# Value products of an attention stage in two column tiles, both halves of the heads together

## The chip, the cores and the metric

One core of one Trainium2 chip runs the whole program. The metric is device time in microseconds (us) of one execution. Engines that matter here: TensorE (PE for its matmuls, PEld for its weight loads), VectorE (DVE), ScalarE (ACT), GpSimd (POOL) and SyncE (SP), which starts the DMA transfers.

## The reference

Three blocks follow each other. The first is a gated linear attention over 2 batches, 8 heads, 768 steps and a head size of 40, given as a recurrence:

```python
C = f_stab * C + i_stab * outer(vt, kt)      # per batch and head, 40x40
n = f_stab * n + i_stab * kt
h_tilde = C @ qt
denom = maximum(abs(n . qt), 1.0)
y[t] = sigmoid(o_gate[t]) * h_tilde / denom
```

The second multiplies each token (320 values) by `w_in` (320x1024) with a ReLU, splits the result into u and v, normalises v over its 512 channels, mixes it over the 768 tokens with `w_spatial`, multiplies by u and then by `w_out`. The third mixes each token with the one before it and applies `w_k`, a squared ReLU, `w_v`, and a sigmoid gate from `w_r`. The two large stages behind the attention don't change here.

## The kernel before, in words

**Attention by chunks.** The 768 steps of each batch are cut into 6 chunks of 128. The 12 chunks are worked one after the other, alternating between the batches (`SEQ`); p, from 0 to 11, is the position in that list. A chunk needs, on TensorE: scores of keys against queries (`sc`, L463), two decay matrices (`ld`, L495 or L471 to L475), the product of the queries with the state carried in (`ip`, L570), the update of that state (`sp`, L533), the value products (`av`, L590), and the transpose of the finished result into the layout of the next block (`tp`, L637). The decay matrix goes through an exponential on ACT and is multiplied by the scores on DVE; that gives `dt`, in halves of 4 heads, 128x512 each.

**Value products.** `intra(i, hh)` does one half. For each of 4 heads a matmul has the head's 128x128 block of `dt` as its weights and streams the value columns of that head. Each head has 41 columns (40 values and a one, for the denominator); the slice taken is three heads wide where there are three, 123 columns, and the columns of the two further heads are overwritten by the matmuls that follow. All eight heads of a chunk write one PSUM bank, `av`, and `normalise` reads it. The operands are f32, and each such matmul stands as two passes in the trace.

**Tiles of the array.** The scores have only 40 rows of contraction. The kernel puts heads 0 to 3 on rows 0 to 39 and heads 4 to 7 on rows 64 to 103, and issues their matmuls alternately (L461 to L464), so that they use two row tiles of the array. All other matmuls of this stage but four very small ones use the array whole.

**Fillers.** The first products of the second block are cut into single matmuls and kept in a list, `fillers`: `vp` (8 matmuls of 512 columns for a chunk, L743) and `up` (32 of 256 columns for two chunks, L748). `pull` puts a chunk's `vp` matmuls at the front of that list once its estimate says that their first weights will be there. `w_v` comes in three pieces, `w_v0` to `w_v2`, each split into a high and a low part by DVE, ACT and POOL.

**The order.** The order of the instructions on TensorE, ACT, DVE and POOL is fixed when the program is built. A planner with a clock of its own walks through the tasks of each position (slots 0 to 6: S0 scores and first half's decays, I, T, N0 first half of the value products, X transpose, S1 second half's decays, N1 second half of the value products and `normalise`). `beat(x)` advances that clock by x. After each task it takes a number of fillers (`FILL`). Where it expects a wait and finds no filler it places `heat`, a matmul on junk (`wp`, L363); `HOT` gives a number of junk matmuls to place at a position without waiting, less the fillers at hand.

The functions that the change touches:

Of the kernel before, what the change touches and what calls it, by code (L numbers as in the profile page):

```python
# [18 lines left out]
def tile_mlstm_gmlp_channelmix(  # L19
# [25 lines left out]
    SEQ = [6 * b + c for c in range(6) for b in range(2)]  # L45
    P = 128
    H, D = 8, 40
    DA = D + 1
# [10 lines left out]
    vec, act, pool, pe = nc.vector, nc.scalar, nc.gpsimd, nc.tensor  # L59
# [11 lines left out]
    clock = [0.0]  # L71
# [12 lines left out]
    class Chain:  # L84
# [14 lines left out]
        def eta(self, k):  # L99
            t = self.ready  # L100
            for s in self.steps:
                t = max(t, free.get(s[0], 0.0)) + s[1] + HOP
                if len(s) > 3 and s[3] == k:
                    break
            return t
# [19 lines left out]
    def use(e, cost, t=None):  # L125
        free[e] = max(free[e], clock[0] if t is None else t) + cost
        return free[e]
# [27 lines left out]
    def beat(cost):  # L155
        clock[0] += cost
        advance(clock[0])
# [170 lines left out]
    st = {}  # L328
# [41 lines left out]
    for a in 'f i d o0 o1 q'.split():  # L370
        dict(f=lambda: sync.dma_start(out=fg, in_=f_gate), i=lambda: sync.dma_start(out=ig, in_=i_gate),
             d=lambda: sync.dma_start(out=id_sb, in_=ident), o=lambda: load_o(int(a[1])), q=lambda: load_qk(SEQ[0]))[a[0]]()
# [207 lines left out]
    def intra(i, hh):  # L580
        if hh == 0:
            both = bank(psa, "at", f"av{i}", ("av", i))
            st["av", i] = both[:, :H * DA].rearrange("p (h d) -> p h d", h=H)
            st["spare", i] = both[:, 384:384 + H]
        wait(("A", i, hh))
        av, vt, A = st["av", i], st["vt", i], st.pop(("A", i, hh))
        for h in range(4):

            own_ = slice(4 * hh + h, min(4 * hh + h + 3, H))
            pe.matmul(av[:, own_, :], A[:, h, :], vt[:, own_, :], start=True, stop=True)  # L590
        beat(0.87)

    def normalise(i):
        b, c = divmod(i, NCH)
# [106 lines left out]
    W = {}  # L701
# [94 lines left out]
    fillers = []  # L796

    vq = []

    def pull():  # L800
        if vq and "v" in W and not (fillers and fillers[0][4]) and eta(["w_v0", ("xt", vq[0])]) <= clock[0] + 1.0:
            fillers[:0] = vpart(vq.pop(0))

    def fill(n, lag=1e9):
# [7 lines left out]
    def wait(*keys):  # L812
        while True:
            gap = eta(keys) - clock[0]
            if gap <= 0.02:
                break
            pull()
            if fillers and eta(fillers[0][2]) <= clock[0] + 0.1:
                fill(1)
            elif warm[0] and gap > 0.2:  # L820
                heat(1)
                clock[0] += 0.08
                advance(clock[0])
            else:
                break
        finish(*keys)
# [38 lines left out]
    for a in 'k0 v0 q6 k6 v1 b v2 n'.split():  # L865
        dict(k=lambda: load_kv(SEQ[a != "k0"]), q=lambda: load_qk(SEQ[1]), n=lambda: load_qk(SEQ[2]),
             v=lambda: w_in_load("u", 0, int(a[1])), b=lambda: load(bm_raw, blockmask[:, 0:3 * DA:DA], 2))[a[0]]()
# [34 lines left out]
                                                            in_=dps[:120, :6 * NCH], func=AF.Exp)))  # L902

    FILL = (6, 4, 1, 3, 1, 1, 1, 4)
    HOT = (0, 1, 0, 0, 3, 2, 0)
    todo = []

    def task(name, fn, keys=(), after=(), slot=0, arrive=None, p=0):
        todo.append(dict(name=name, fn=fn, keys=keys, after=set(after), slot=slot, arrive=arrive, p=p))

    def position(p):
        i = SEQ[p] if p < NT else None
        n = SEQ[p + 1] if p + 1 < NT else None
        nn = SEQ[p + 2] if p + 2 < NT else None
        prev = SEQ[p - 1] if p else None

        def s0():
            if p == 3:
                w_in_split("v")
            if p == 7:  # L920
                wsp_half(0, lsp_[0])
            scores(n, 0)
            logd(n, 0)
            if p % 2 == 0 and 2 <= p < NT - 2:
                gate_rows(p // 2 + 1)

        def gates():
            wait(("G1", 0))
            gate_exp("c", 96, G1)
            decays()  # L930

        def st_():
            if p == 2:
                finish(("eg", "c"), ("dec", 0), stall=False)
                gp.release()
                lsp_.append(tc.alloc_tile_pool(name="lsp", bufs=1, side="left", reuse_waits="tile"))
                vec.tensor_scalar(out=omu_sb, in0=mu_sb, scalar1=-1.0, scalar2=1.0, op0=ALU.mult, op1=ALU.add)
            state(i)

        def tr():  # L940
            turn(prev)
            vq.append(prev)
            if p % 2 == 0:
                fillers.extend(upart(p // 2 - 1))

        def s1():
            scores(n, 1)
            logd(n, 1)
            if p + 3 < NT:
                load_qk(SEQ[p + 3])  # L950
            if p in (3, 5):
                finish(("e", n, 0), ("e", n, 1), stall=False)
                open_gate(2 if p == 3 else 4)
                open_gate(3 if p == 3 else 5)
                use("A", 2.6)

        def n1():
            intra(i, 1)
            normalise(i)
            if nn is not None:  # L960
                load_kv(nn)
            if p == 0:
                w_in_load("v", 1, 0)
                sync.dma_start(out=mu_sb, in_=mu)
            if p == 1:
                w_in_load("v", 1, 1)
                load_o(2)
                load_o(3)
            if p == 2:
                w_in_load("v", 1, 2)  # L970
                load_o(4)
            if p == 3:
                load_o(5)
            if n is not None:
                key_weights(n)

        if n is not None:
            task(("S0", n), s0, after=[("N1", prev), ("S1", i)], arrive=n, slot=0, p=p)
        if p == 0:
            task("B", lambda: (wait(("G0", 1)), gate_exp("b", 16, GC[1])), [("G0", 1)], slot=7, p=p)  # L980
        if p == 2:
            task("G", gates, [("G1", 0)], p=p, slot=7)
        if i is not None:
            c = i % NCH
            if c > 0:
                task(("I", i), lambda: inter(i), [("C", i - 1)], [("N1", prev)], slot=1, p=p)
            if c < NCH - 1:
                task(("T", i), st_, [("kw", i)], [("I", i), ("N1", prev)] + ["G"] * (p >= 2), slot=2, p=p)
            task(("N0", i), lambda: intra(i, 0), [("A", i, 0)], [("S0", i), ("N1", prev)], slot=3, p=p)
        if prev is not None:  # L990
            task(("X", prev), tr, [("x", prev)], [("N1", prev), ("X", SEQ[p - 2] if p > 1 else None)], slot=4, p=p)
        if n is not None:
            task(("S1", n), s1, after=[("S0", n)], slot=5, p=p)
        if i is not None:
            task(("N1", i), n1, [("A", i, 1)], [("N0", i), ("I", i), ("T", i), ("S1", n), ("X", SEQ[p - 2] if p > 1 else None)], slot=6, p=p)

    lsp_ = []
    for p in range(NT + 1):
# [5 lines left out]
    while todo:  # L1004
        p = todo[0]["p"]
# [26 lines left out]
        passed.add(best["name"])  # L1032
        hot = HOT[p] if p < len(HOT) else 0
        if best["slot"] < 7:
# [315 lines left out]
```

## Time and profile before

| what | value |
|---|---|
| median of 3 runs | 307.42 us (305.56 to 309.02) |
| profiled execution | 305.26 us |
| its span, first to last instruction | 303.5 us |
| PE busy | 295.1 us, 2020 matmul passes |
| ACT, DVE, POOL busy | 172.5, 217.4, 139.4 us |
| attention stage with fillers | up to about 112 us of the span |
| value products | 192 passes, 12.6 to 108.4 us |

A matmul's recorded time is its latency; matmuls overlap, so what a pass costs is read from the distance between starts. The chain of waits is followed back from the last instruction: where a row of it names PE, nothing but PE's own queue set the time there. "Granted clock" is the share of TensorE's full clock.

### The profile page before, as it was taken

The page shows a single profiled execution, that of the slowest core. Times are in us where ns is not written, and L with a number is a line of the kernel's source. Part 1 is how long each engine was busy: PE and PEld are TensorE (multiplying, and loading weights), DVE is VectorE, ACT ScalarE, POOL GpSimd, SP SyncE. Part 2 cuts the span into 40 slices and gives each one's busy share as a digit, 9 for nine tenths or more (in the row PEclk, how much of TensorE's full clock was granted, in tenths as well). Part 3 has the DMA queues.
Part 4 walks back from the last instruction along what each step waited for, and adds up shares of the span by engine and source line. Part 5 has one row for each costly group of instructions (what it writes and reads, how often), then busy time and mean ns, then how long its engine had stood idle before and what let it go on. Part 6 is the DMA issues. An engine that isn't in the chain of part 4 may idle for free.

```text
span 303.5 us, 5569 instructions
## 1 busy us (share of the span) xinstructions
PE 295.1 (97%) x2020; PEld 280.5 (92%) x2020; DVE 217.4 (72%) x440; ACT 172.5 (57%) x383; POOL 139.4 (46%) x167
## 2 busy tenths in 40 slices
PE   8998998998999999999999999999999999999994
PEld 6887986887889989999999999999999999999994
DVE  7869997656787768566789989898766665654601
ACT  4675596787655446633354644686926835825600
POOL 5234445447777655615647527485415305303500
PEclk9999999999999999999999999999999999999998
DMA  5979754333343301463124303321010010010001
GB/s 162 305 216 314 245 179 144 82 107 115 94 141 107 107 2 44 128 213 123 43 71 154 114 1 89 92 81 46 1 65 2 0 45 22 0 45 22 1 24 44
DMA packets 13939, 28.76 MB, mean 95 GB/s; under 512 B 2407, under 2 KB 7783, under 8 KB 13911
## 3 DMA queue, kind: packets, MB, share of 16 engines
q1 hardware_dynamic: 13879, 28.33, 29.9%
q8 instruction: 16, 0.26, 0.3%
q0 software_dynamic: 32, 0.07, 0.2%
q14 instruction: 12, 0.10, 0.1%
HBM read 26.20 MB, written 1.97 MB: 93 GB/s over the span
## 4 chain that ended last, share of the span: by engine, by line
PE 87%; ACT 4%; DVE 4%; issue 2%; POOL 1%; DVEq 0%; POOLq 0%; ACTq 0%
PE spp L662 16%; PE kp L662 15%; PE vv L662 14%; PE wop L662 7%; PE up L662 7%; PE vp L662 6%; PE rp L662 5%; PE av L590 5%; PE sc L463 3%; PE wp L363 3%; PE ip L570 2%; PE sp L533 1%; PE ld L495 1%; PE tp L637 1%; ACT vr L731 1%
## 5 line engine op out<-in xcount | busy, mean ns | idle before, releaser
L1193 POOL TENSOR_TENSOR sq<-sq 128x384 f32<-128x384 f32 x32 | 29.9, 941 | 47.9 <-ACT sq L1192 47.9
L662 PE MATMUL spp<-wsp,vn 128*128 128x384 f32 x288 | 50.4, 334 | 0.0
L662 PEld LDWEIGHTS spp<-wsp,vn 128*128 128x128 f32 x288 | 49.9, 188 | 0.0
L662 PE MATMUL kp<-xk,wk 128*128 128x384 f32 x256 | 45.3, 334 | 0.0
L662 PEld LDWEIGHTS kp<-xk,wk 128*128 128x128 f32 x256 | 44.5, 188 | 0.0
L662 PE MATMUL vv<-wv,k 128*128 128x320 f32 x288 | 42.9, 309 | 0.0
L662 PEld LDWEIGHTS vv<-wv,k 128*128 128x128 f32 x288 | 42.4, 188 | 0.0
L235 DVE TENSOR_TENSOR k<-sq,k 128x384 fp32r<-128x384 f32 x32 | 26.2, 820 | 13.6 <-ACT k L1194 13.6
L662 PE MATMUL up<-xg,w_u 128*128 128x256 f32 x192 | 32.4, 297 | 0.0
L1090 POOL TENSOR_TENSOR vs<-vs,u 128x384 f32<-128x384 f32 x16 | 19.5, 1221 | 23.4 <-DVE vs L1089 22.0
L662 PE MATMUL vp<-w_v,xg 128*128 128x512 f32 x96 | 28.5, 415 | 0.5 <-POOL w_v L235 0.5
L662 PEld LDWEIGHTS up<-xg,w_u 128*128 128x128 f32 x192 | 26.1, 191 | 0.4
L1192 ACT ACTIVATE sq<-kp 128x384 f32<-128x384 f32 x32 | 15.5, 488 | 16.8 <-PE kp L662 14.8
L590 PE MATMUL av<-kvq,dt 128*128 128x123 f32 (+1 forms) x192 | 24.6, 272 | 0.0
L590 PEld LDWEIGHTS av<-kvq,dt 128*128 128x128 f32 x192 | 23.8, 191 | 0.7
L284 DVE SCALAR_TENSOR_TENSOR wbits<-wsq,wbits 128x320 int32<-128x320 int32 (+1 forms) x27 | 20.0, 741 | 4.5 <-ACT wsq L274 3.4
L662 PE MATMUL wop<-gt,wo 128*128 128x384 f32 x128 | 22.8, 334 | 0.0
L662 PEld LDWEIGHTS wop<-gt,wo 128*128 128x128 f32 x128 | 22.2, 188 | 0.0
L1233 DVE TENSOR_TENSOR ob<-rs,vv 128x320 f32<-128x320 f32 x12 | 5.8, 487 | 20.4 <-PE vv L662 19.4
L662 PEld LDWEIGHTS vp<-w_v,xg 128*128 128x128 f32 x96 | 17.1, 190 | 3.4 <-POOL w_v L235 0.8
L288 DVE SCALAR_TENSOR_TENSOR wsq<-wraw,wbits 128x320 int32<-128x320 int32 (+1 forms) x21 | 19.7, 944 | 0.4
L1091 ACT CAST gt<-vs 128x384 fp32r<-128x384 f32 x16 | 8.2, 513 | 17.7 <-POOL vs L1090 17.6
(184 smaller groups left out, 567.2 us busy)
## 6 DMA issues: line engine op xcount, KB each, us to landing
kvq<-in_kvq_dram SPq DMA_DIRECT2D x10, 516.0 KB
qk<-in_qk_dram SPq DMA_DIRECT2D x24, 160.0 KB
wraw<-in_w_k_dram SPq DMA_DIRECT2D x6, 512.0 KB
wraw<-in_w_v_dram SPq DMA_DIRECT2D x8, 320.0 KB
wraw<-in_w_sp_dram SPq DMA_DIRECT2D x12, 192.0 KB
og<-in_o_tok_dram SPq DMA_DIRECT2D x12, 160.0 KB
out_dram<-ob SPq DMA_DIRECT2D x12, 160.0 KB
w_inu<-in_w_in_dram SPq DMA_DIRECT2D x3, 512.0 KB
```

Source lines behind the costliest of these rows:

```text
L235: eng.tensor_tensor(out=out, in0=a, in1=b.bitcast(F32), op=ALU.subtract)
L284: vec.scalar_tensor_tensor(out=t["bits"], in0=t["sq"].bitcast(I32), scalar=3, in1=t["bits"], op0=ALU.logical_shift_left, op1=ALU.bitwise_or)
L288: vec.scalar_tensor_tensor(out=t["sq"].bitcast(I32), in0=t["high"], scalar=SIGN, in1=t["bits"], op0=ALU.bitwise_and, op1=ALU.bitwise_or)
L363: pe.matmul(wp[:, :256], junk[:, :P], junk, start=True, stop=True)
L463: pe.matmul(st["sc", i, x][:, h * P:(h + 1) * P], k_[64 * x:64 * x + D, h, :], q_[64 * x:64 * x + D, h, :], start=True, stop=True)
L570: pe.matmul(ip[:, h0 * DA:(h0 + n) * DA], qt[:n * D, g, :], cs[:n * D, h0 * DA:(h0 + n) * DA], start=True, stop=True)
L590: pe.matmul(av[:, own_, :], A[:, h, :], vt[:, own_, :], start=True, stop=True)
L662: pe.matmul(out[0], l, x, start=j == 0, stop=j == len(prs) - 1)
L1090: ("P", 1.29, lambda: pool.tensor_tensor(out=vs, in0=vs, in1=ut[b][:, d, sl], op=ALU.mult)),
L1091: ("A", 0.51, lambda: act.copy(gt[:, 0], vs)), ("V", 0.7, lambda: sub(vec, gt[:, 1], vs, gt[:, 0])))
L1192: chain(("k2", g, f), ("A", 0.49, lambda: act.activation(out=sq, in_=ps, func=AF.Relu), ("kp", g, f)), ("P", 0.96, lambda: pool.tensor_ten ...
L1193: ("P", 0.96, lambda: pool.tensor_tensor(out=sq, in0=sq, in1=sq, op=ALU.mult)),
```

## The change

From position 3 on, N0 only takes the PSUM bank; the products of both halves are issued in N1, 4 heads and then 4 heads. At every position a head's block of weights is cut into two halves of 64 columns, which go to two column tiles of the array (the outputs at partitions 0 and 64), and the slice that is streamed is 60 columns wide instead of 123 (41 for the last head). `pull` waits for all three pieces of `w_v`, with a margin of 0.2 instead of 1.0. `HOT` asks for two junk matmuls at position 2.

```diff
@@ intra
             st["spare", i] = both[:, 384:384 + H]
+            if SEQ.index(i) >= 3:
+                return
+        elif SEQ.index(i) >= 3:
+            wait(("A", i, 0), ("A", i, 1))
+            products(i, 0)
         wait(("A", i, hh))
-        av, vt, A = st["av", i], st["vt", i], st.pop(("A", i, hh))
-        for h in range(4):
-
-            own_ = slice(4 * hh + h, min(4 * hh + h + 3, H))
-            pe.matmul(av[:, own_, :], A[:, h, :], vt[:, own_, :], start=True, stop=True)
-        beat(0.87)
+        products(i, hh)
+
+    def products(i, hh):
+        av, vt, A = st["av", i].rearrange("p h d -> p (h d)"), st["vt", i].rearrange("p h d -> p (h d)"), st.pop(("A", i, hh))
+        for h in range(4 * hh, 4 * hh + 4):
+
+            own_ = slice(h * DA, min(h * DA + 60, H * DA))
+            for r in (0, 64):
+                pe.matmul(av[r:r + 64, own_], A[:, h % 4, r:r + 64], vt[:, own_], start=True, stop=True)
+        beat(0.6)
@@ pull
-        if vq and "v" in W and not (fillers and fillers[0][4]) and eta(["w_v0", ("xt", vq[0])]) <= clock[0] + 1.0:
+        if vq and "v" in W and not (fillers and fillers[0][4]) and eta(["w_v0", "w_v1", "w_v2", ("xt", vq[0])]) <= clock[0] + 0.2:
@@
-    HOT = (0, 1, 0, 0, 3, 2, 0)
+    HOT = (0, 1, 2, 0, 3, 2, 0)
@@ position
-            task(("N1", i), n1, [("A", i, 1)], [("N0", i), ("I", i), ("T", i), ("S1", n), ("X", SEQ[p - 2] if p > 1 else None)], slot=6, p=p)
+            task(("N1", i), n1, [("A", i, 0), ("A", i, 1)], [("N0", i), ("I", i), ("T", i), ("S1", n), ("X", SEQ[p - 2] if p > 1 else None)], slot=6, p=p)
```

The order on TensorE changes with it. First place: a late position, the fillers being `up`. Before, from the last filler ahead of the first half of the value products to the end of the second:

```order
L662 MATMUL up_1_1220<-xg_681,w_u_149 128x256
L590 MATMUL av_1247<-kvq_1047,dt_0_1087 128x123 x4
L662 MATMUL up_2_1258<-xg_681,w_u_148 128x256
L662 MATMUL up_2_1258<-xg_681,w_u_149 128x256
L662 MATMUL up_2_1258<-xg_681,w_u_148 128x256
L637 MATMUL tp_1263<-id_sb,x_1170 128x128 x3
L662 MATMUL up_2_1258<-xg_681,w_u_148 128x256
L495 MATMUL ld_1_1275<-rl,lt_91 128x512
L662 MATMUL up_2_1258<-xg_681,w_u_149 128x256
L590 MATMUL av_1247<-kvq_1047,dt_1_1153 128x123 x2
L590 MATMUL av_1247<-kvq_1047,dt_1_1153 128x82
L590 MATMUL av_1247<-kvq_1047,dt_1_1153 128x41
```

Now, the same stretch of such a position:

```order
L671 MATMUL up_2_1322<-xg_715,w_u_148 128x256
L671 MATMUL up_2_1322<-xg_715,w_u_149 128x256
L671 MATMUL up_3_1351<-xg_715,w_u_148 128x256
L671 MATMUL up_3_1351<-xg_715,w_u_149 128x256
L646 MATMUL tp_1359<-id_sb,x_1265 128x128 x3
L671 MATMUL up_3_1351<-xg_715,w_u_148 128x256
L495 MATMUL ld_1_1365<-rl,lt_91 128x512
L671 MATMUL up_3_1351<-xg_715,w_u_148 128x256
L599 MATMUL av_1348<-kvq_1129,dt_0_1169 64x60 x8
L599 MATMUL av_1348<-kvq_1129,dt_1_1236 64x60 x6
L599 MATMUL av_1348<-kvq_1129,dt_1_1236 64x41 x2
```

The first half has moved behind the transpose and the second decay matrix, and eight whole-array matmuls have become sixteen of 64 output rows, in one run.

Second place: position 4. Before, from the state update `sp` to the fillers at its end:

```order
L533 MATMUL sp_760<-kvq_586,kw_717 120x123 x2
L533 MATMUL sp_760<-kvq_586,kw_717 80x82
L590 MATMUL av_765<-kvq_586,dt_0_626 128x123 x4
L637 MATMUL tp_778<-id_sb,x_710 128x128 x3
L495 MATMUL ld_1_783<-rl,lt_91 128x512
L497 LDWEIGHTS mask
L497 MATMUL ld_1_783<-mask 128x512
L590 MATMUL av_765<-kvq_586,dt_1_690 128x123 x2
L590 MATMUL av_765<-kvq_586,dt_1_690 128x82
L590 MATMUL av_765<-kvq_586,dt_1_690 128x41
L662 MATMUL vp_721<-w_v_602,xg_388 128x512
L662 MATMUL vp_721<-w_v_603,xg_388 128x512
```

Now, from the last of the junk behind `sp` to the first fillers:

```order
L363 LDWEIGHTS id_sb
L363 MATMUL wp<-id_sb 128x256
L646 MATMUL tp_836<-id_sb,x_759 128x128 x3
L495 MATMUL ld_1_848<-rl,lt_91 128x512
L497 LDWEIGHTS mask
L497 MATMUL ld_1_848<-mask 128x512
L599 MATMUL av_831<-kvq_630,dt_0_686 64x60 x8
L599 MATMUL av_831<-kvq_630,dt_1_725 64x60 x6
L599 MATMUL av_831<-kvq_630,dt_1_725 64x41 x2
L671 MATMUL up_0_886<-xg_715,w_u_148 128x256
L671 MATMUL up_0_886<-xg_715,w_u_149 128x256
```

Three junk matmuls stand before `sp` and six between `sp` and `tp`, where none stood; the six `vp` matmuls that stood at the ends of positions 3 and 4 have moved to position 5 and later, and `up` of the next two chunks takes their place.

In the whole program the junk matmuls go from 56 to 77: five more ahead of the first `tp` and one fewer behind it, eight more at position 2 (four of them ahead of `sp`), nine at position 4.

## Rows read from the trace of the kernel before

**Rows 1.** The page, busy time, share of the span and instructions of each engine.

```profile
PE 295.1 (97%) x2020; PEld 280.5 (92%) x2020; DVE 217.4 (72%) x440; ACT 172.5 (57%) x383; POOL 139.4 (46%) x167
```

**Rows 2.** The page, the chain that ended last, by engine.

```profile
PE 87%; ACT 4%; DVE 4%; issue 2%; POOL 1%; DVEq 0%; POOLq 0%; ACTq 0%
```

**Rows 3.** Stages: start:end, length, busy us (instructions) by engine, granted clock, DMA, GB/s.

```profile
60.40:70.10 9.70, 9.70 (x73) 8.30 (x72) 4.95 (x18) 8.23 (x16) 4.69 (x7) 1.00 0.31 88
88.40:96.70 8.30, 8.30 (x71) 7.71 (x70) 6.85 (x20) 5.24 (x15) 6.38 (x11) 1.00 0.40 125
```

**Rows 4.** The chain, one late position: start us, length us, what.

```profile
88.51 1.09 PE sc L463 x16
89.60 0.43 PE ld L495
...
94.97 0.23 PE ld L495
```

**Rows 5.** PEld's timeline, same position: start, length, line, operands, count.

```profile
88.44 0.97 PEld L463 LDWEIGHTS sc<-qk 40*128 40x128 f32 x16 [0.35 <-issue]
...
92.99 0.98 PEld L590 LDWEIGHTS av<-kvq,dt 128*128 128x128 f32 x8
93.89 0.42 PEld L662 LDWEIGHTS up<-xg,w_u 128*128 128x128 f32 x3
...
95.05 0.97 PEld L590 LDWEIGHTS av<-kvq,dt 128*128 128x128 f32 x8
95.94 0.66 PEld L662 LDWEIGHTS up<-xg,w_u 128*128 128x128 f32 x5
```

**Rows 6.** PEld's timeline, the last load of 80 columns and the next.

```profile
92.81 0.15 PEld L533 LDWEIGHTS sp<-kvq,kw 128*80 128x80 f32 x1
92.88 0.19 PEld L662 LDWEIGHTS up<-xg,w_u 128*128 128x128 f32 x1
```

**Rows 7.** Groups by shape: count, busy us, mean ns of one, idle before.

```profile
L590 PE MATMUL av<-kvq,dt 128*128 128x123 f32 x144 | 20.1, 275 | 0.0
L590 PE MATMUL av<-kvq,dt 128*128 128x41 f32 x24 | 4.2, 262 | 0.0
```

**Rows 8.** Loads by shape, same columns.

```profile
L590 PEld LDWEIGHTS av<-kvq,dt 128*128 128x128 f32 x192 | 23.8, 191 | 0.7
L533 PEld LDWEIGHTS sp<-kvq,kw 128*80 128x80 f32 x20 | 2.5, 149 | 0.0
```

**Rows 9.** The chain, positions 1 and 2, and its return to PE.

```profile
18.36 1.09 PE wp L363 x7
...
20.24 0.48 ACT xg L651
...
29.32 0.80 PE sp L533 x6
```

**Rows 10.** ACT's timeline, the copy that the first `tp` waits for.

```profile
18.96 0.24 ACT L619 COPY x<-x 128x64 f32<-128x64 f32 x1 [0.17 <-DVE x L615]
```

**Rows 11.** PE's timeline: matmuls that waited, with idle time and releaser.

```profile
29.32 0.80 PE L533 MATMUL sp<-kvq,kw 128*120 128x123 f32 x6 [1.44 <-ACT dt L479]
...
47.02 0.47 PE L495 MATMUL ld<-rl,lt 128*128 128x512 f32 x1 [0.56 <-DMA rl<-Lxc]
...
49.33 0.73 PE L662 MATMUL vp<-w_v,xg 128*128 128x512 f32 x2 [0.48 <-POOL w_v L235]
...
72.17 0.49 PE L495 MATMUL ld<-rl,lt 128*128 128x512 f32 x1 [0.88 <-ACT dt L505]
```

**Rows 12.** The chain where it leaves PE between 54 and 72 us.

```profile
54.83 0.60 ACT vr L731
...
71.62 0.51 ACT dt L505
```

**Rows 13.** PE's timeline, the matmuls beside the loads of Rows 5.

```profile
93.11 1.05 PE L590 MATMUL av<-kvq,dt 128*128 128x123 f32 x8
```

**Rows 14.** The chain behind the attention stage.

```profile
126.86 24.96 PE spp L662 x144
```

## The prediction

> **What bounds the kernel now.** I read the engine totals first: PE is busy for 295.1 of 303.5 us, and no other engine is near it [rows 1]. The chain of waits says the same from the other side: 87% of it is PE [rows 2]. So what PE no longer has to do is gained, unless another engine takes over. The stage view shows where that could be: between 88.4 and 96.7 us PE is busy for the whole stage and ACT for 5.24 of 8.30 us, but between 60.4 and 70.1 us ACT has 8.23 of 9.70 [rows 3], and there the chain does leave PE and runs through ACT, from 54.83 to the end of an exponential at 72.13 [rows 12]. It is also off PE, on ACT and DVE, from 20.24 to 29.32 [rows 9]. From 72.17 us to the end no wait on PE of more than 0.2 us stands in its timeline. What follows is unchanged from the spatial product on, which starts at 126.86 [rows 14], when the attention stage and its fillers are through. The granted clock is 1.00 in the stages shown [rows 3].
>
> **What a value product costs now.** The loads of eight passes start at 92.99 and the next matmul's load at 93.89: 0.90 us, 0.112 for a pass. The second half, which ends with slices of 82 and 41 columns, takes 95.94 - 95.05 = 0.89 [rows 5]. A pass with 41 columns is no nearer to the next than one with 123, so it is the load of 128 weight columns that sets the pace; the recorded length of the matmul hardly moves either, 262 against 275 ns [rows 7]. Narrower streams alone would give nothing. A position costs 0.90 + 0.89 = 1.79 us.
>
> **What two tiles can do.** Column tiles occur nowhere in this trace; the nearest rows are the scores, in two row tiles. Their 16 loads take 0.97 us, as long as 8 loads of the whole array, 0.98 [rows 5]: two tiles work side by side, a pair every 0.111 us. They also show what a change of tiling costs: on the chain the scores hold 1.09 us [rows 4], 0.20 more than 8 x 0.111, and the decay matmul behind them holds 0.43 where the one without a change before it holds 0.23 [rows 4]. In and out together cost 0.40 us.
>
> A half block has 64 weight columns. A load of 80 columns is followed by the next after 0.07 us [rows 6], and lasts 149 ns against 191 for 128 [rows 8]; by the first, 64 columns take 0.056 us; by the second, 0.112 - 64 x 42/48 ns = 0.056. The 0.07 is rounded and stands for 0.065 to 0.075, so for 0.052 to 0.060; I take 0.058 us for a pair of passes, if the two column tiles work side by side as the row tiles do. Lower end: 0.052. Upper end: 0.111, the pair of the scores.
>
> - From position 3 on: 16 pairs x 0.058 + 0.40 = 1.33 us for 1.79, a gain of 0.46, nine times: **-4.1 us**.
> - Positions 0 to 2 keep their halves apart and pay the change of tiling twice: 8 x 0.058 + 0.40 = 0.86 for 0.89 or 0.90. Six times: **-0.2 us**. Without the merging of the halves, in other words, the tiles would bring nothing.
>
> **What is given back.** A junk matmul costs 1.09 / 7 = 0.16 us [rows 9], and there are 21 more of them.
> - Five more ahead of the first `tp` and one fewer behind it, 0.6 us. The chain passes this junk and goes on through ACT [rows 9]; the `tp` stands behind the junk and waits for a copy on ACT that ended at 18.96 + 0.24 = 19.20 [rows 10], just before the seventh junk matmul was through, so the added ones can be on the path. I take half: **+0.3**.
> - Four at position 2 ahead of `sp` lie in its wait of 1.44 us [rows 11], which ACT and DVE set: 0. Four behind it, where the chain is back on PE: **+0.6**.
> - Nine at position 4: 1.4 us. They stand where PE waited 0.56 us for a DMA of decay rows, and the six `vp` matmuls that waited 0.48 us for `w_v` have left [rows 11]. These are done later and cost the same there. 1.4 - 0.56 - 0.48: **+0.4**.
> - Positions 5 and 6 give 2 x 0.46 us to a PE that arrives earlier at the wait of 72.17 us, which ACT ends after 0.88 us [rows 11]. ACT's chain [rows 12] stays, and `vp`, with its work on ACT, comes a position later, into the same stretch. I let half be lost: **+0.45**.
>
> The products of the first half now come later, and `normalise` with them only after both; it began behind the second half before too, so nothing on DVE, POOL or in the loads of the next chunk is queued behind a later start. The bank `av` is taken at the same place and freed by the same instruction. The transfers keep their order.
>
> Sum: -4.1 - 0.2 + 0.3 + 0.6 + 0.4 + 0.45 = -2.5 us. The profiled execution took 305.26 us, 303.5 of it span, and lies 2.2 us below the median of 307.42; it would come to 302.8, and against the median I forecast **304.9 us**, -0.8%.
>
> **A rule against it.** The loads of the value products run inside the matmuls before them, on the same 128 rows: loads from 92.99 for 0.98 us [rows 5], matmuls from 93.11 for 1.05 [rows 13]. The Trainium skill, page "TensorE: Matmul & The Clock Gate", section "Part 3: Packing small matmuls — row/col tiling", says that a load overlaps matmuls in flight only where its row group differs from theirs. The two column tiles share all their rows, so that by it a load would stand between the streams. The row just named does not bear the rule out for the whole array; no run here shows it for column tiles. It is the third rival.
>
> **The rivals.**
> 1. Nothing is lost to ACT or to the junk at position 1, and the pairs go at 0.054. For it: PE's timeline has long stretches without a wait, and the order is new around 72 us. Then 0.75 us less is given back and 192 pairs save 0.004 each, 0.8 us: -4.0, **303.4 us**. Chance 0.23.
> 2. The other engines absorb it. For it: ACT at 8.23 of 9.70 us [rows 3], and three `vp` sums pushed into positions 6 and 7. Against: from 80 us on PE alone is on the chain. If positions 3 to 7 give nothing, 5 x 0.46 less the 0.45 already counted, 1.85 us, are lost: -0.7, **306.7 us**. Chance 0.18.
> 3. The tiles don't load side by side. Then 32 passes at 0.058 follow each other: 1.86 + 0.40 = 2.26 for 1.79, +0.47 nine times, and 1.33 for 0.90 in six halves, +0.43 each, together +6.8; with the junk and less of the ACT loss, +8. With pairs at the scores' 0.111 it is 16 x 0.111 + 0.40 = 2.18, +0.39 nine times and +0.39 six times: +5.9, with the junk +7. **About 314 us.** It decides from a pair of 0.072 us on: 192 pairs x 0.0135 use up the 2.5 us. For it: no column tile in the trace. Against: the row tiles, and loads that run under matmuls today. Chance 0.20.
>
> **How the numbers follow.** The forecast has 0.39. A measurement of this kernel can tell about 1%, 3.1 us, from no change. Of the forecast's cases three in ten lie beyond -3.1 us (a pair of 0.055, or half of the give-backs absent), and all of rival 1: faster 0.35. The rest of the forecast and rival 2: same 0.44. Rival 3 and a small part of rival 2: slower 0.21. The range leaves out rival 3. Its low end is rival 1 at 303.4 less the 1.9 us by which the fastest of the three runs lay below the median: 301.5. Its high end is rival 2 with the 1.6 us by which the slowest lay above, and half a us more of junk on the path: 309.
>
> **What would show it.** In the changed profile, loads of the value products should come in pairs a few ns apart, the pairs 0.055 to 0.06 us apart, and the 32 passes of a position should hold 1.1 to 1.2 us on the chain with about 0.2 more on the matmul behind them. A distance of 0.11 us between pairs, or single loads at 0.06, is rival 3. `vp` should no longer wait for `w_v`; a wait on ACT between 65 and 90 us that is longer than 0.88 us is rival 2. The start of the spatial product, 126.86 us now, should come at about 124.4. A granted clock below 1.00 anywhere behind the first few us would make all of this wrong.

## The result and the profile after

The changed kernel takes **308.82 us** (median of 20 runs, 306.29 to 311.15), the kernel before 306.43 (20 runs, 305.56 to 309.02). The ratio is 1.0053, 95% interval 1.0031 to 1.0075: about 1.6 us slower, where 0.8% faster was forecast. The ratio leaves out the two slowest of the 20 runs, 310.99 and 311.15 us, and lies near the quotient of the means of the rest (308.4 and 306.8 us), below that of the two medians. The profiled execution took 308.54 us, with a span of 305.5.

The page, engine totals and the chain by engine:

```profile
PE 294.4 (96%) x2233; PEld 273.3 (89%) x2233; DVE 218.5 (72%) x440; ACT 172.4 (56%) x383; POOL 140.3 (46%) x167
...
PE 71%; DVE 9%; ACT 6%; POOL 5%; DMA 4%; issue 2%; SPq 1%; POOLq 0%; DVEq 0%; ACTq 0%
```

PE has hardly less to do than before and 16 points less of the chain [rows 1, 2]; DVE, ACT, POOL and DMA have taken them. The value products themselves did what was predicted. The chain at a late position (start, length, what):

```profile
97.83 0.23 PE ld L495
98.07 0.12 PE up L671
98.19 1.06 PE av L599 x32
99.25 0.78 PE up L671 x5
100.03 1.09 PE sc L463 x16
```

And the weight loads there, with the loads of both tiles in one row of 32:

```profile
98.11 1.01 PEld L599 LDWEIGHTS av<-kvq,dt 128*64 128x64 f32 x32 [0.25 <-DVE sb L732]
```

Within that row the two loads of a pair start 7 to 8 ns apart and the pairs 0.058 us apart. The 32 passes hold the chain for 1.06 us; the same products held PE for 0.90 + 0.89 us before. So the two column tiles load and stream side by side, and rival 3 is out: its rule, quoted in the prediction from the Trainium skill (page "TensorE: Matmul & The Clock Gate", section "Part 3: Packing small matmuls — row/col tiling"), doesn't hold for column tiles in this trace.

What has changed are the waits. PE's timeline (idle time and releaser in brackets), to be held against [rows 11]:

```profile
27.38 0.48 PE L471 MATMUL ld<-unit,Axb 128*128 128x512 f32 x1 [0.59 <-DVE dt L489]
29.50 0.30 PE L423 MATMUL gpsc<-id_sb,i 96*128 96x96 f32 x1 [0.71 <-DVE i L416]
32.27 0.80 PE L533 MATMUL sp<-kvq,kw 128*120 128x123 f32 x6 [1.22 <-ACT dt L479]
48.29 0.49 PE L363 MATMUL wp<-id_sb 128*128 128x256 bf16 x3 [0.85 <-ACT u L764]
...
77.24 0.50 PE L671 MATMUL vp<-w_v,xg 128*128 128x512 f32 x1 [0.95 <-ACT vr L740]
...
91.64 0.50 PE L671 MATMUL vp<-w_v,xg 128*128 128x512 f32 x1 [0.65 <-ACT u L764]
```

The waits on `w_v` and on the decay rows are gone, and so is the one at 72.17. In their place stand two new ones between 27 and 30 us, and three on ACT's work for the second block (`u`, and `vr` for the normalised half v). The state update of position 2, the first `sp` above, starts at 32.27 instead of 29.32. Part of that is the start of this execution: the first scores stand at 10.12, before at 9.16. Counted from the first scores the update comes 22.2 us later, before 20.2.

That distance, and the one from this update to the first matmul of the spatial product, are what the experiments are read by ("head" and "tail", us, both read from PE's timeline). The clock is the mean granted clock of the profiled execution. Where it is below 0.995 that trace holds a stretch of 3 to 7 us at TensorE's lower level, 1.2 GHz, between 29 and 38 us (e4 a second one from 119 us on); in the others the clock stands at 2.4 GHz from 7 us on until the last few us. "Clock up" counts the runs with a mean granted clock of 0.995 or more, and gives their median less the median of such runs of the kernel before on the same chip (41 of its 75 runs on four chips); for the changed kernel those of its chip are not known.

| kernel | median us | ratio to before, interval | head | tail | clock | clock up: runs, us |
|---|---|---|---|---|---|---|
| before | 306.43 | 1 | 20.2 | 97.4 | 0.997 | 41 of 75 |
| changed | 308.82 | 1.0053 (1.0031 to 1.0075) | 22.2 | 96.7 | 1.000 | 8 of 20 |
| e1 tiles only | 306.58 | 0.9999 (0.9967 to 1.0031) | 20.2 | 96.5 | 0.997 | 2 of 12, -1.0 |
| e3 changed, 0.87 | 303.29 | 0.9905 (0.9869 to 0.9940) | 19.6 | 95.6 | 0.998 | 6 of 6, -2.7 |
| e4 changed, old `pull` | 311.80 | 1.0159 (1.0110 to 1.0208) | 21.2 | 103.8 | 0.981 | 2 of 6, +3.2 |
| e5 changed, no junk at 2 | 308.69 | 1.0067 (1.0039 to 1.0096) | 21.6 | 99.0 | 0.989 | 0 of 7 |
| e10 0.6 early only | 307.56 | 1.0023 (0.9994 to 1.0052) | 21.9 | 95.6 | 0.999 | 4 of 12, 0.0 |
| e11 0.6 late only | 304.23 | 0.9905 (0.9876 to 0.9935) | 19.6 | 96.6 | 0.998 | 6 of 6, -1.9 |
| e12 e3 on the whole array | 306.41 | 0.9982 (0.9962 to 1.0001) | 20.0 | 97.6 | 1.000 | 12 of 12, +0.3 |
| e13 e3, no junk at 2 | 303.19 | 0.9884 (0.9854 to 0.9914) | 19.7 | 95.6 | 0.999 | 5 of 6, -3.0 |
| e14 before with 0.6 | 313.84 | 1.0240 (1.0218 to 1.0262) | 21.8 | 103.2 | 0.987 | 0 of 5 |
| e15 e13, halves apart | 306.12 | 0.9968 (0.9938 to 0.9997) | 18.9 | 97.1 | 1.000 | 5 of 12, -1.9 |
| e16 e13, no junk at 4 | 303.92 | 0.9914 (0.9889 to 0.9939) | 19.4 | 96.7 | 0.994 | 3 of 6, -2.9 |
| e17 e3, five more junk | 304.12 | 0.9920 (0.9897 to 0.9942) | 20.1 | 95.5 | 1.000 | 6 of 6, -2.0 |
| e18 e10 with 8 junk for 12 | 306.96 | 0.9998 (0.9973 to 1.0023) | 21.5 | 97.8 | 0.988 | 7 of 12, -0.4 |

Each ratio is against the kernel before on the same chip; 0.001 of it is 0.31 us. Differences between two kernels below are differences of such ratios; their intervals are some 0.003 to 0.005, 1.0 to 1.7 us, to either side. A ratio mixes two things: what the kernel needs at one clock, and how often its clock falls. The last column shows the first by itself, from few runs in some rows.

### The profile page after: what moved, and what is told of

The parts are those of the page before. It is cut to its first block, busy times and chain, and to the rows that moved or that the text cites. A ratio compares the mean times of both kernels' runs of the same rounds, so it can differ in the third digit from the quotient of the medians.

```text
span 305.5 us, 6000 instructions
## 1 busy us (share of the span) xinstructions
PE 294.4 (96%) x2233; PEld 273.3 (89%) x2233; DVE 218.5 (72%) x440; ACT 172.4 (56%) x383; POOL 140.3 (46%) x167
## 4 chain that ended last, share of the span: by engine, by line
PE 71%; DVE 9%; ACT 6%; POOL 5%; DMA 4%; issue 2%; SPq 1%; POOLq 0%; DVEq 0%; ACTq 0%
PE spp L671 16%; PE kp L671 15%; PE vv L671 14%; PE wop L671 7%; PE up L671 5%; PE rp L671 5%; DMA bm_raw<-in_blockmask_dram 3%; PE vp L671 2%; DMA qk<-in_qk_dram 2%; POOL vn L235 2%; PE sc L463 1%; DVE sb L728 1%; DVE dt L508 1%; PE av L599 1%; SPq L216 1%
## 5 line engine op out<-in xcount | busy, mean ns | idle before, releaser
L671 PE MATMUL up<-xg,w_u 128*128 128x256 f32 x192 | 31.0, 295 | 0.0
L284 DVE SCALAR_TENSOR_TENSOR wbits<-wsq,wbits 128x320 int32<-128x320 int32 (+1 forms) x27 | 20.9, 774 | 4.4 <-ACT wsq L274 3.5
L671 PEld LDWEIGHTS wop<-gt,wo 128*128 128x128 f32 x128 | 22.2, 188 | 0.0
L235 POOL TENSOR_TENSOR vn<-vr,vn 128x512 fp32r<-128x512 f32 x12 | 15.4, 1287 | 6.8 <-ACT vn L750 6.8
L288 DVE SCALAR_TENSOR_TENSOR wsq<-wraw,wbits 128x320 int32<-128x320 int32 (+1 forms) x21 | 17.2, 821 | 0.3
L1141 DVE SCALAR_TENSOR_TENSOR tm<-x,mu_sb,tm 128x384 f32<-128x384 f32 x24 | 17.1, 748 | 0.0
```

Of the source, the lines that this page charges most:

```text
L235: eng.tensor_tensor(out=out, in0=a, in1=b.bitcast(F32), op=ALU.subtract)
L284: vec.scalar_tensor_tensor(out=t["bits"], in0=t["sq"].bitcast(I32), scalar=3, in1=t["bits"], op0=ALU.logical_shift_left, op1=ALU.bitwise_or)
L288: vec.scalar_tensor_tensor(out=t["sq"].bitcast(I32), in0=t["high"], scalar=SIGN, in1=t["bits"], op0=ALU.bitwise_and, op1=ALU.bitwise_or)
L671: pe.matmul(out[0], l, x, start=j == 0, stop=j == len(prs) - 1)
L1141: return lambda: vec.scalar_tensor_tensor(out=t[:, c], in0=x[:, c, 1:], scalar=mu_sb[:, w, c:c + 1], in1=t[:, c], op0=ALU.mult, op1=ALU.add)
```

## The experiments

### The tiles alone (e1)

```diff
 # before, intra: halves apart, beat(0.87), old pull, old HOT
-            own_ = slice(4 * hh + h, min(4 * hh + h + 3, H))
-            pe.matmul(av[:, own_, :], A[:, h, :], vt[:, own_, :], start=True, stop=True)
+            own_ = slice(h * DA, min(h * DA + 60, H * DA))
+            for r in (0, 64):
+                pe.matmul(av[r:r + 64, own_], A[:, h % 4, r:r + 64], vt[:, own_], start=True, stop=True)
```

(the loop over the heads and the views of `av` and `vt` change with it, as in `products` above)

> The kernel before with nothing but the value products in column tiles of 60 columns; halves apart, order on all engines as before. Theory A (the products are cheaper, and what is lost comes from the new order): a block of 4 heads costs 8 pairs of 0.058 us and some 0.23 for the change of tiling, 0.70 instead of 0.89; 18 blocks lie where PE is on the chain, so 18 x 0.19 = 3.4 us less, of which the wait on ACT at 72 us may take back 0.8: a ratio of 0.989 to 0.993 to the kernel before. Theory B (column tiles cost the time by themselves: less work on TensorE lets its clock fall in some executions): ratio 1.00 or above, with mean granted clocks below 0.995 in several executions.

No difference in the ratio, 0.9999. The chain at a late position, before:

```profile
93.27 0.89 PE av L590 x8
94.16 0.36 PE up L662 x3
...
96.81 1.09 PE sc L463 x16
```

and in e1:

```profile
88.69 1.09 PE sc L463 x16
...
93.46 0.61 PE av L591 x16
94.07 0.55 PE up L663 x3
...
96.81 1.09 PE sc L463 x16
```

A half's 16 passes hold 0.61 us instead of 0.89, the way into the column tiles included (8 pairs alone are 0.46), but the three fillers behind them hold 0.55 instead of 0.36. So two thirds of what a half saves go into its change of tiling, and about 0.1 us is left: from scores to scores 8.12 us, where the kernel before needs 8.30 (88.51 to 96.81 [rows 4]). The tail is 0.9 us shorter, and the two runs with the clock up are 1.0 us faster than such runs of the kernel before. The ratio shows none of this, because the clock was below 0.995 in 10 of the 12 runs, against 7 of 18 of the kernel before on the same chip. Theory B named this, and the prediction's sentence that without the merging the tiles bring nothing is right for the ratio only. Why the clock falls more often here is not shown: DVE, ACT and POOL work in the same order as before, and in the kept trace the clock didn't fall.

### The planner's figure (e3)

```diff
 # the changed kernel
-        beat(0.6)
+        beat(0.87)
```

> The changed kernel with the planner told 0.87 us for four heads, as before, instead of 0.6. Theory A (the shorter figure let the planner move the splits of the first weights ahead of the gate steps on DVE and ACT at positions 1 and 2, which start the state update of position 2 later): that update starts 1.3 us or more earlier than in the changed kernel relative to the first value product, and the ratio to before falls from 1.005 to 0.995 or less. Theory B (clock): as the changed kernel, 1.003 to 1.008. Theory C (the first vp sums come too late): as the changed kernel.

0.9905: 4.5 us faster than the changed kernel, and faster than the kernel before by 2.9 us (1.8 to 4.0). Nothing that TensorE computes for the result differs; there are four junk matmuls fewer, 73 instead of 77. What matters can be seen where the head was lost. DVE's timeline of the changed kernel, from the copy `xg` to the scan (L410) of the gate steps, on which position 2 depends:

```profile
21.70 0.73 DVE L235 TENSOR_TENSOR xg<-tp,xg 128x256 fp32r<-128x256 f32 x2 [0.61 <-ACT xg L660]
22.46 0.69 DVE L288 SCALAR_TENSOR_TENSOR wsq<-w_inu,wbits 128x512 int32<-128x512 int32 x1
23.78 0.69 DVE L284 SCALAR_TENSOR_TENSOR wbits<-wsq,wbits 128x512 int32<-128x512 int32 x1 [0.62 <-ACT wbits L278]
24.39 1.36 DVE L407 TENSOR_TENSOR f<-f,m 96x128 f32<-96x128 f32 x1
...
26.18 0.42 DVE L410 TENSOR_TENSOR_SCAN f<-ones,f 96x128 f32<-96x128 f32 x1
```

The same with 0.87:

```profile
22.45 0.73 DVE L235 TENSOR_TENSOR xg<-tp,xg 128x256 fp32r<-128x256 f32 x2 [1.82 <-ACT xg L660]
23.22 0.69 DVE L284 SCALAR_TENSOR_TENSOR wbits<-wsq,wbits 128x512 int32<-128x512 int32 x1
23.83 0.28 DVE L407 TENSOR_TENSOR f<-f,m 96x128 f32<-96x128 f32 x1
...
24.55 0.42 DVE L410 TENSOR_TENSOR_SCAN f<-ones,f 96x128 f32<-96x128 f32 x1
```

From `xg` to the scan it is 4.48 us against 2.10. The planner, told that a half block takes 0.6, expects a longer gap on PE and puts more of the splits of `w_u` into it. A step of one split (L288) now stands ahead of the gate steps, and the next one behind it waits 0.62 for ACT, which itself waited for POOL's part of the split. ACT's timeline:

```profile
22.52 0.68 ACT L274 ACTIVATE wsq<-w_inu 128x512 f32<-128x512 f32 x1 [0.85 <-POOL w_u L235]
```

Up to the first gate step (L407) this makes 2.69 - 1.38 = 1.31 us. Then that step, two inputs of 96x128, takes 1.36 us instead of 0.28. POOL's timeline beside it:

```profile
24.33 1.27 POOL L235 TENSOR_TENSOR w_u<-wsq,w_u 128x512 fp32r<-128x512 f32 x1 [1.85 <-ACT w_u L297]
```

It starts 0.06 us before the gate step, and the step ends 0.15 us after it. That is the other 1.08. The same step takes 1.36 or 1.37 us in all six traces with 0.6 at positions 0 to 2 (changed, e4, e5, e10, e14, e18) and 0.28 in the nine others.

### The later pull (e4)

```diff
 # the changed kernel
-        if vq and "v" in W and not (fillers and fillers[0][4]) and eta(["w_v0", "w_v1", "w_v2", ("xt", vq[0])]) <= clock[0] + 0.2:
+        if vq and "v" in W and not (fillers and fillers[0][4]) and eta(["w_v0", ("xt", vq[0])]) <= clock[0] + 1.0:
```

> The changed kernel with the old condition for taking vp: first piece of w_v, margin 1.0. Theory C (waiting for all of w_v pushes three vp sums and their work on ACT, DVE and POOL into positions 6 to 8, where PE then waits 0.95 and 0.65 us): the ratio falls from 1.005 to about 1.000 and the waits between 72 and 92 us shrink. Theory A or B: no gain; PE waits for w_v again at position 5, 0.5 to 1 us, ratio 1.005 to 1.010.

3.2 us slower than the changed kernel, more than either theory expected. PE's timeline has three waits on `w_v` in place of the one of [rows 11], and longer ones behind them:

```profile
52.41 0.73 PE L671 MATMUL vp<-w_v,xg 128*128 128x512 f32 x2 [0.43 <-POOL w_v L235]
54.97 0.50 PE L671 MATMUL vp<-w_v,xg 128*128 128x512 f32 x1 [0.39 <-POOL w_v L235]
57.53 0.97 PE L671 MATMUL vp<-w_v,xg 128*128 128x512 f32 x3 [0.33 <-POOL w_v L235]
...
74.35 0.39 PE L671 MATMUL up<-xg,w_u 128*128 128x256 f32 x1 [1.40 <-ACT vr L740]
...
118.44 0.88 PE L646 MATMUL tp<-id_sb,x 128*128 128x128 f32 x3 [1.83 <-DVE x L624]
```

The later pull is a gain in the changed kernel, not a move of the same cost. Part of the 3.2 us may be clock: this trace holds two stretches at 1.2 GHz, and the two runs with the clock up are only 1.9 us above those of the changed kernel (309.2 against 307.25).

### The junk at position 2 (e5)

```diff
 # the changed kernel
-    HOT = (0, 1, 2, 0, 3, 2, 0)
+    HOT = (0, 1, 0, 0, 3, 2, 0)
```

> The changed kernel with no junk asked for at position 2 (eight junk matmuls fewer). Cost of the junk: four of the eight stand on the chain, so if they only cost time the ratio falls by 0.002, to 1.003. Theory B (clock): without them the clock falls in more executions, the mean granted clock drops below that of the changed kernel, and the ratio rises to 1.008 or more.

No difference from the changed kernel in time. The granted clock was 0.987 to 0.992 in all seven runs; with the junk it was 0.998 or more in 8 of 20. The profiled execution by windows (start:end, length, then PE, PEld, DVE, ACT and POOL, granted clock, DMA):

```profile
28.00:32.00 4.00, 1.64 (x11) 1.41 (x11) 2.68 (x8) 1.75 (x6) 1.66 (x3) 0.85 0.77 290
32.00:36.00 4.00, 4.00 (x31) 3.65 (x31) 2.08 (x7) 1.33 (x4) 1.10 (x2) 0.50 0.28 83
36.00:40.00 4.00, 4.00 (x38) 3.38 (x39) 2.26 (x7) 1.05 (x4) 0.80 (x1) 0.80 0.27 46
```

PE was busy for 1.64 of the first 4 us, and from 30.8 to 37.6 us the clock stood at 1.2 GHz, though PE had work without a break from 31.7 us on. In the changed kernel's profiled execution PE had 2.34 us of work in the first window, and no fall:

```profile
28.00:32.00 4.00, 2.34 (x18) 1.63 (x17) 2.84 (x9) 1.23 (x3) 1.66 (x3) 1.00 1.02 327
32.00:36.00 4.00, 3.73 (x52) 3.28 (x52) 2.77 (x8) 2.43 (x8) 1.66 (x2) 1.00 0.51 164
```

So this junk seems to keep the clock up in some executions (the clock fell in 7 of 7 runs without it, in 12 of 20 with it), and costs about what that saves: at a fallen clock the runs without it are about half a us faster (308.7 against 309.2).

### The figure at the early and at the late positions (e10, e11)

```diff
 # the changed kernel; e10, and e11 with the two numbers exchanged
-        beat(0.6)
+        beat(0.87 if SEQ.index(i) >= 3 else 0.6)
```

> The changed kernel, with the planner told 0.6 us for a block only at positions 0 to 2, and 0.87 from position 3 on. Theory (the smaller figure costs its time through the order it gives ACT, DVE and POOL before the state update of position 2): as slow as the changed kernel, 308.5 us (307.3 to 310), with the update at 31.5 to 32.5 us and more than 1 us of wait ahead of it. Rival (the figure hurts in the later positions, where the waits at 77.24 and 91.64 us stand): 303.5 us (302.5 to 304.8), as with 0.87 everywhere. If both stretches count, about 306.

> The mirror of the run before: 0.87 at positions 0 to 2, 0.6 from position 3 on. Theory (early order): 303.3 us (302.3 to 304.6), the level of 0.87 everywhere, granted clock at 0.998 or more. Rival (later positions): 308.5 us (307 to 310), with the wait near 77 us back. If both count, about 306.

Early alone costs 3.6 us over e3: its head is 21.9 with a tail of 95.6, and 8 of its 12 runs had a granted clock of 0.988 to 0.994. With the clock up it is 2.7 us over e3: that is delay, and the rest is clock. Late alone has the ratio of e3 (and a median 0.9 us above it), with a tail of 96.6 instead of 95.6 and two of the changed kernel's waits, this one first:

```profile
74.67 0.50 PE L671 MATMUL vp<-w_v,xg 128*128 128x512 f32 x1 [1.02 <-ACT vr L740]
```

So the late part is worth about 0.9 us (4.5 less 3.6, and the distance of the two medians), and the ratio of e11, equal to that of e3, doesn't separate it from nothing.

### What the tiles bring where the halves are together (e12)

```diff
 # e3, products()
-            own_ = slice(h * DA, min(h * DA + 60, H * DA))
-            for r in (0, 64):
-                pe.matmul(av[r:r + 64, own_], A[:, h % 4, r:r + 64], vt[:, own_], start=True, stop=True)
+            own_ = slice(4 * hh + h, min(4 * hh + h + 3, H))
+            pe.matmul(av[:, own_, :], A[:, h, :], vt[:, own_, :], start=True, stop=True)
```

(the loop over the heads and the views of `av` and `vt` are those of the kernel before, too)

> 0.87 everywhere, halves together, later pull, junk at position 2, but the value products on the whole array again, eight passes of 0.112 us for a half: what the column tiles bring by themselves. Theory (the products' sum holds: 9 x 0.46 and 6 x 0.04 us on PE's own path): 4.3 us over the version with tiles, 307.6 us (306.6 to 308.6). Rival (PE's waits absorb most of it): 304.5 us (303.5 to 305.5).

2.4 us over e3 (1.1 to 3.6), between the two expectations; with the clock up in both it is 3.0. Where PE alone sets the time the sum holds. The chain of e12:

```profile
90.26 1.09 PE sc L463 x16
...
96.28 1.71 PE av L598 x16
98.00 0.67 PE up L670 x5
98.66 1.09 PE sc L463 x16
```

And of e3:

```profile
89.21 1.09 PE sc L463 x16
...
95.26 1.06 PE av L599 x32
96.32 0.78 PE up L671 x5
97.10 1.09 PE sc L463 x16
```

8.40 us from scores to scores against 7.89: 0.51 gained, after the fillers behind the products have given back 0.11 for the change of tiling. But from 70.28 to 80.27 us e3 needs 9.99, and e12 for the same position 10.01. PEld's timeline of e3 shows why:

```profile
74.64 0.19 PEld L671 LDWEIGHTS vp<-w_v,xg 128*128 128x128 f32 x1 [0.46 <-ACT vr L740]
...
79.13 0.30 PEld L671 LDWEIGHTS vp<-w_v,xg 128*128 128x128 f32 x2 [0.23 <-ACT xg L660]
79.59 0.30 PEld L671 LDWEIGHTS vp<-w_v,xg 128*128 128x128 f32 x2 [0.16 <-DVE xg L235]
```

e12 has none of these three waits. At position 4 the junk waits 0.85 us for `u` in e3 and 0.31 in e12; that position is not shorter with tiles either. Position 8 is only 0.1 us shorter.

### The junk without the smaller figure (e13, e16)

```diff
 # e3, then e16
-    HOT = (0, 1, 2, 0, 3, 2, 0)
+    HOT = (0, 1, 0, 0, 3, 2, 0)   # e13
+    HOT = (0, 1, 0, 0, 0, 2, 0)   # e16
```

> 0.87 everywhere, tiles, halves together, later pull, but no junk at position 2: the prediction charged this junk 0.6 us. Theory (it keeps the clock up across the waits around 25 to 31 us, and the early order being the old one, the wait ahead of the state update stays near 1.4 us): the granted clock is below 0.995 in most executions, 304.8 us (303.8 to 306). Rival (it only costs its own time): 302.7 us (302 to 303.4), clock at 0.998 or more.

> Column tiles, halves together, 0.87, later pull, no junk at position 2 and none at position 4 either (nine matmuls of 0.16 us fewer). By the prediction's term of +0.4 us for them: 302.8 us (302.2 to 303.4). If all nine were on PE's path, 1.4 us less: 301.8. If they kept the clock up: 304 us or more, with the granted clock below 0.995.

For e13 the theory missed and the rival held: the clock was at 0.998 or more in five of six runs without the junk, at 303.19 us. With the head short again the junk may have little to protect; that is argued, not tested. e13 has the lowest ratio (0.9884); its 0.6 us below e3 lie inside both intervals. The nine junk matmuls of position 4 cost nothing that shows: without them (e16) PE waits 1.14 us for the decay rows and the time is, within the intervals, the same; with the clock up it is -2.9 against -3.0 us. The clock fell in three of e16's six runs and in one of e13's, too few to tell.

### The figure alone, on the kernel before (e14)

```diff
 # before
-        beat(0.87)
+        beat(0.6)
```

> The kernel before, with nothing changed but the planner's figure, 0.6 us for a half block instead of 0.87: whole-array products, halves apart. Theory (the figure itself reorders the other engines and delays the state update of position 2 by 2.2 us and the later positions by about 1 us, and the granted clock falls in more executions): 310 us (308.5 to 312), the update 22 us or more behind the first scores (20.1 before). Rival (the figure only hurts together with the tiles or the merged halves): 307 us (306 to 308).

7.4 us slower, more than any expectation: not one product has changed, and the head is 21.8 us. All five runs had the clock at about 0.987, and in the profile PE is busy for 1.64 us of 28 to 32 and at 1.2 GHz behind it:

```profile
28.00:32.00 4.00, 1.64 (x12) 1.34 (x11) 2.68 (x8) 1.69 (x6) 1.66 (x3) 0.84 0.94 358
32.00:36.00 4.00, 4.00 (x20) 3.91 (x20) 1.72 (x6) 1.26 (x4) 1.17 (x2) 0.50 0.30 89
```

The old `pull` adds to it: the tail has waits on `w_v` of 0.51 and 0.89 us. The figure by itself does the harm; the later pull hides part of it in the changed kernel (e4), and the junk keeps some of its executions at the full clock (e5).

### The halves apart (e15)

```diff
 # e13, intra()
-            if SEQ.index(i) >= 3:
-                return
-        elif SEQ.index(i) >= 3:
-            wait(("A", i, 0), ("A", i, 1))
-            products(i, 0)
...
-            task(("N1", i), n1, [("A", i, 0), ("A", i, 1)], ...
+            task(("N1", i), n1, [("A", i, 1)], ...
```

> Column tiles, 0.87, later pull, no junk at position 2, but the two halves apart again at every position. The prediction says that without the merging the tiles bring nothing: 9 x 0.42 us more than the same kernel with the halves together, 307 us (306 to 308). Rival (the tiles alone brought nothing in the earlier run because of the old pull): 304 us (303 to 305).

2.6 us over e13, less than the 3.8 of the sum. More than half of it is clock: it was below 0.995 in 7 of the 12 runs, and in one of e13's six. With the clock up e15 is 1.1 us over e13, and 1.9 us faster than the kernel before; those five runs, at a median of 304.3, lie at the rival's time and not at the theory's. The rival's reason, that the old `pull` hid what the tiles bring, isn't shown: e1 has the old one and gains 1.0 us with the clock up. So the merging is worth some 1.1 us at one clock, and the tiles with the later pull bring something without it. How much of that the pull alone brings is untested.

### Junk or order at position 1 (e17, e18)

```diff
 # e17: e3, the other engines' order kept
+        if best["name"] == ("X", SEQ[0]):
+            heat(5)
+            clock[0] -= 5 * 0.107
         best["fn"]()
```

```diff
 # e18: e10, the planner's clock kept, 8 junk matmuls instead of 12
-                heat(1)
+                if first["name"] == ("X", SEQ[0]):
+                    few.append(0)
+                if len(few) > 7 and first["name"] == ("X", SEQ[0]):
+                    clock[0] += 0.107
+                else:
+                    heat(1)
```

> The version with 0.87 everywhere, and five more junk matmuls ahead of the first transpose, placed without moving the planner's clock, so that every other engine keeps its order: one of the two things that the smaller figure did at position 1. Theory (the order on ACT, DVE and POOL, not this junk, makes the delay): 303.6 us (302.8 to 304.4), the state update of position 2 at most 0.5 us later behind the first scores than with 0.87 alone (19.6 us). Rival (the junk delays the transpose and so the update): 305.5 us or more, the update 21.5 us behind the first scores.

> 0.6 at positions 0 to 2 and 0.87 behind, as in an earlier run, with the planner's clock and the order on ACT, DVE and POOL exactly as there, but eight junk matmuls instead of twelve ahead of the first transpose: the reordering of the other engines without most of the added junk. Theory (their order makes the delay): 306.8 us (305.6 to 308), the update of position 2 at 21.4 us or more behind the first scores, granted clock below 0.995 in a third or more of the executions. Rival (junk ahead of the transpose makes it, and only the planner's clock kept it from showing in the run that added five): 304 us (303 to 305), the update at 20 us.

The smaller figure does two things at position 1: five more junk matmuls, and splits ahead of the gate steps. In the traces DVE, ACT and POOL work through e17 in the order of e3, and through e18 in that of e10. The junk alone gives a head of 20.1 (0.5 more) and a time that the intervals don't separate from e3. The order, with one junk matmul more than e3 ahead of the first `tp`, gives 21.5 (1.9 more) and 2.8 us over e3 (2.3 with the clock up). So it is the order on DVE, ACT and POOL.

## Why the prediction was wrong

**The step that failed** is the sentence "nothing on DVE, POOL or in the loads of the next chunk is queued behind a later start". It looked at what the later products delay and not at what the planner does with a changed `beat`. The figure 0.6 was counted only as junk ahead of the first `tp`. That junk was sized fairly (+0.3 forecast, 0.5 of head in e17). The splits that came with it were not in the sum: 1.9 us of head (e18), and a granted clock of 0.986 to 0.994 in 12 of 20 runs, which in the traces of e5, e14 and e18 is a stretch at 1.2 GHz at the end of this head. Together with the late positions this is 4.5 us (e3), of which 3.6 belong to positions 0 to 2 (e10). The prediction had named a granted clock below 1.00 as what would overturn it; it gave no reason to expect one. That 308.82 us still lies below the 309 at the high end of the range is luck: that end was rival 2 with its scatter and more junk on the path, not this delay.

**Without that figure the forecast's -2.5 us was near**: e3 has -2.9, and the sum without the junk of position 1 would be -2.8. That is partly luck: terms were wrong in both directions and nearly made up for each other.

- *The products, -4.3.* Pace (0.058 us a pair) and gain where PE alone is on the chain (0.51 against 0.46) were right. The way in and out cost less than the 0.40 taken: about 0.13 in the 1.06 us, and 0.11 behind. Over all positions e12 to e3 gives 2.4, or 3.0 with the clock up.
- *The loss to ACT, +0.45.* Mis-sized: 1.3 to 1.9 of the 4.3 don't arrive. It was put at positions 5 and 6, before the wait of 72.17, which is gone; most of it is found at position 4 (`u`) and at position 7 (`vr`, `xg`). Rival 2 was this, and its sign, a wait on ACT over 0.88 us between 65 and 90, is the one of 0.95 at 77.24 in the changed kernel.
- *The `vp` sums, "done later and cost the same there".* They cost less there: with the old pull the changed kernel is 3.2 us slower (e4), 1.9 in the two runs with the clock up.
- *The junk at 2 and at 4, +0.6 and +0.4.* At 2: 0.6 between e3 and e13, not more than the intervals; at 4: nothing measurable (e16).

That the tiles bring nothing without the merging (0.04 us a half) held for the ratio of e1, but not for its reason: a half gains 0.1 us at a late position, and it is the clock that falls more often. In e15, with the later pull beside them, tiles and pull together bring 1.0 us (0.9968), and 1.9 with the clock up. Of the signs listed, `vp` no longer waits for `w_v`, and in the chain the spatial product starts at 129.17 instead of the 124.4 that was hoped for.

**Open.** What decides whether the clock falls in an execution of the same kernel isn't settled, nor why it falls more often with the halves apart in column tiles (e1, e15). PE's work from 28 to 32 us was 1.64 us in two executions with a fall and 2.34 in the changed kernel's without; in e18 the fall came at 29.3 us, inside this stretch, so that its 2.82 us say nothing. No run took POOL's split away from the gate step alone; its 1.08 us is read from the rows. The later pull by itself, on the kernel before, was not run either.

## What to carry to other kernels

A number by which a planner places work is part of the schedule: when a block gets shorter, correcting its figure reorders every engine, so compare all engines' queues, not only the one that was changed, and try the old figure too. A gain on the bounding engine counts only at the positions where no other engine's chain is as long: price it position by position. Where the clock falls in some runs and not in others, compare runs at one clock as well: the ratio alone made the tiles of e1 look worthless. The version with the lowest ratio here keeps the tiles, the merged halves and the later pull, with 0.87 and without the junk at position 2 (e13: 0.9884, 0.9854 to 0.9914).

## What was not expected of the hardware

A two-input operation of DVE on 96x128 values that starts while POOL works on a two-input operation ends 0.15 us after POOL's, when both of its inputs lie in SBUF. The gate step above is one case (0.28 us alone, 1.36 beside POOL). The kernel before has another, an operation that also takes 0.28 us alone; DVE's timeline:

```profile
25.03 0.80 DVE L235 TENSOR_TENSOR Axc<-i,Axc 96x128 fp32r<-96x128 f32 x1
```

and POOL's:

```profile
24.88 0.80 POOL L605 TENSOR_TENSOR og<-og,nn 128x320 f32<-128x320 f32 x1 [4.73 <-ACT nn L610]
```

POOL ends at 25.68, DVE at 25.83; in e3 the same two end at 26.99 and 27.14. A step with one input in PSUM is not held up: in the changed kernel's trace the one at 18.70 us (L621, 128x8) takes 0.17 us inside POOL's operation from 18.54 to 19.36. A larger operation ends later behind POOL's: in the same trace a split step (L284) of 128x512 that starts at 44.52 us, beside POOL, takes 1.32 us instead of 0.68 and ends 0.55 us after it. The Trainium skill (page "SBUF — State Buffer", section "Who interferes with whom") says that a DVE instruction with two inputs in SBUF contends with a GpSimd instruction that reads SBUF, that the lock is exclusive, and that the order of issue decides which of the two blocks. These pairs agree with it.
